# Second dense product cut 384 + 256 columns in place of 512 + 128, with two 256-wide pieces to a PSUM bank

## The chip, the cores and the metric

One core of one Trainium2 chip. The metric is the device time of one execution in microseconds. Engines are written as the profile writes them: PE is the tensor engine, PEld its weight loads, DVE the vector engine, ACT the scalar engine.

## The reference

A gate mixes two branches over 2048 tokens of 640 features: a state-space layer (branch A) and a two-layer perceptron (branch B). Only the last line of branch B is touched here.

```python
g = sigmoid((x * gate_w).sum(-1, keepdims=True))
a = state_space(x, ...)                       # two complex products and a scan over time
h = gelu(x @ w1 + b1)                         # 640 -> 1728: first dense product
b = h @ w2 + b2                               # 1728 -> 640: second dense product
out = g * a + (1 - g) * b                     # bfloat16, 1 x 2048 x 640
```

## The kernel before

The tokens are taken in four chunks of 512, each of four tiles of 128 tokens. PE runs the products of the chunks one after the other in a fixed order; ACT and DVE keep up beside it. In the second dense product the weight tile (the stationary operand) is a 128 x 128 piece of the hidden activations, `gel`, and `w2` streams past it. The matmuls write into banks of PSUM that the program allocates 512 columns wide, and none of them writes more, so the 640 output columns are taken in two pieces. There are 13 full contraction blocks of 128 and a last one of 64 rows, which is done in `half_rows` with two 64-row matmuls side by side.

```python
MAIN, REST = (0, 512), (512, D)               # D = 640

def biased(c, kind, i):                       # ACT writes the bias b2 into a PSUM bank ahead of the product
    p = bank()                                # one of 8 banks, in rotation
    d0, d1 = MAIN if kind == "wide" else REST
    n = 1 if kind == "wide" else H            # H = 2: two REST pieces share a bank
    ...
    nc.scalar.activation(out=v, in_=src, func=ACT.Identity)
    act(0.6 if n == 1 else 0.4)               # the scheduler's own clock; it only decides the order of issue
    opened[c, kind, i] = p

def first_banks(c):                           # called before the product in front ends
    biased(c, "wide", 0)
    biased(c, "wide", 1)

def fin_b(c, at={}):
    def full(p, col, a, d0, d1):
        for kf in range(KF - 1):              # 13 blocks
            nc.tensor.matmul(p[:, col:col + d1 - d0], lhsT=gel[c][:, kf, a * P:(a + 1) * P],
                             rhs=w2_sb[:, kf, d0:d1], start=False, stop=False, skip_group_check=True)
            pe(d1 - d0)
    def out_of(p, col, a, d0, d1):            # eviction by ACT, times (1 - g)
        ...
    def half_rows(): ...                      # the last 64 rows, all four tiles, once per chunk
    biased(c, "rest", 0)
    biased(c, "wide", 2)
    for h in range(2):
        for j in range(H):
            a = h * H + j
            full(opened[c, "wide", a], 0, a, *MAIN)
            if a == 0:
                biased(c, "wide", 3)
                biased(c, "rest", 1)
            if h == 1:
                out_of(opened[c, "wide", a], 0, a, *MAIN)
            ...
        for j in range(H):
            full(opened[c, "rest", h], j * P, h * H + j, *REST)
        if h == 0:
            half_rows()
            ...                               # evictions of the wide pieces
        ...                                   # evictions of the rest pieces
```

`full` is line 598, `half_rows` 614, `biased` 587, `out_of` 606. The changed kernel has one line more, so there they are 599, 615, 588 and 607. Three words: the third product is the last one of a chunk (line 657, the states of the scan times C); a seed is a DVE write of x times D into a bank ahead of it (line 573); a fold is a one-off scaling of C.

## Time and profile before

| | |
|---|---|
| time, median of 3 runs | 215.77 us (215.67 to 216.65) |
| PE / DVE / ACT busy | 98% / 88% / 48% |
| granted PE clock (share of full speed) | 1.0 |
| matmuls at line 598, mean distance of starts | 215.8 to 216.0 ns (512 wide), 55.8 ns (128 wide) |
| the second dense product (lines 598 and 614) | 28% of the chain that ended last |

First the engine line of the page, and the two lines of the chain that ended last: the work followed back from the last instruction, at each step to what released it (shares of the span, by engine and by line).

```profile
PE 210.0 (98%) x1385; PEld 116.4 (54%) x1385; DVE 188.4 (88%) x385; ACT 103.3 (48%) x185; POOL 1.1 (0%) x12
...
PE 96%; DMA 2%; SPq 0%; ACT 0%; DVE 0%; issue 0%
PE bank L598 27%; PE bank L258 26%; PE bank L657 20%; PE bank L540 20%; DMA xn<-in_A_x_dram 2%; PE bank L614 1%; PE bank L284 1%; PE bank L223 0%; SPq L122 0%; ACT xT L232 0%; DVE ot L662 0%; PE bank L361 0%; PE bank L274 0%; PE bank L390 0%
```

A busy PE alone says little, since matmul records overlap. The chain says more: nearly all of the time is PE following itself. The next lines are PE's waits in the trace before (total us, times, longest): 1.5 us in all, every one in the first 8 us.

```profile
PE bank L220 <- PEq L716: 0.8, 1, 0.8
PE bank L361 <- ACT xT L232: 0.3, 1, 0.3
PE bank L223 <- DMA xn<-in_A_x_dram: 0.2, 1, 0.2
PE bank L258 <- DVE xT L230: 0.2, 1, 0.2
```

Now the chain in order of time (start us, length us, what, number of instructions) around the products of the last chunk.

```profile
185.69 7.06 PE bank L598 x52
192.76 0.65 PE bank L614 x8
193.41 7.17 PE bank L598 x52
200.58 10.90 PE bank L657 x90
```

Fifty-two matmuls of the second product (26 of 512 columns, 26 of 128) take 7.06 us, so a pair takes 271.5 ns. Last, the groups by shape: busy us, mean ns of one, then idle time before them.

```profile
L598 PE MATMUL bank<-w_sb,gel 128*128 128x512 bf16 x208 | 46.2, 379 | 0.0
L598 PEld LDWEIGHTS <-gel 128*128 128x128 bf16 x416 | 32.3, 98 | 25.5
L598 PE MATMUL bank<-w_sb,gel 128*128 128x128 bf16 x208 | 12.9, 219 | 0.0
L606 ACT ACTIVATE gb<-bank,gcol 128x512 f32<-128x512 f32 x16 | 10.6, 686 | 30.3 <-PE bank L614 17.3 <-PE bank L598 12.9
L587 ACT ACTIVATE bank<-b2bc 128x512 f32<-128x512 bf16 x16 | 9.1, 599 | 6.1 <-DVE ot L662 6.1
L606 ACT ACTIVATE gb<-bank,gcol 128x128 f32<-128x128 f32 x16 | 5.0, 368 | 3.2 <-PE bank L598 3.2
L587 ACT ACTIVATE bank<-b2bc 128x256 f32<-128x256 bf16 x8 | 3.1, 389 | 1.2 <-DVE ot L662 1.2
```

A weight load shows 98 ns. A 128-wide matmul starts 55.8 ns after the one before it, and each has a load of its own. But 98 ns is how long one load's record is, not how often loads can follow each other: matmuls with a load each did follow each other at 55.8 ns (200 distances, all 55 or 56), with no idle time before them. (The starts are taken from the instruction records of the trace.)

### The profile page before, as it was taken

To read this page: it belongs to the slowest core of one execution; us is meant where nothing else is said; L and a number is where in the kernel's file an instruction comes from. 1 tells how busy PE (TensorE), PEld (TensorE's weight loads), DVE (VectorE), ACT (ScalarE), POOL (GpSimd) and SP (SyncE) were. 2 spreads that over 40 slices of the span, in tenths; PEclk is the share of its full clock that TensorE was granted. 3 is DMA by queue.
4 is the path that set the end of the run, shared out by engine and by line. 5 is a ranking of instruction groups with operands and counts; after the bars stand their busy time and mean duration, and the time that the engine had idled before them with its cause. 6 is when DMAs were issued, how large, how long until landed. Compare 5 with 4: busy or idle time off the path is not lost.

```text
span 214.2 us, 3547 instructions
## 1 busy us (share of the span) xinstructions
PE 210.0 (98%) x1385; PEld 116.4 (54%) x1385; DVE 188.4 (88%) x385; ACT 103.3 (48%) x185; POOL 1.1 (0%) x12
## 2 busy tenths in 40 slices
PE   7999999999999999999999999999999999999994
PEld 3745444454454644775445577444455567664773
DVE  2899999999998999998999999899999999973153
ACT  3599956675867697203573210456682422304200
POOL 1000000000000000000000000000000000000000
PEclk9999999999999999999999999999999999999999
DMA  6899999995000000061000006100000000100011
GB/s 200 238 189 182 187 250 314 257 212 136 3 0 0 3 0 2 12 186 62 0 0 3 0 0 185 63 0 0 2 3 14 0 3 31 61 34 0 0 66 61
DMA packets 31059, 15.84 MB, mean 74 GB/s; under 512 B 22978, under 2 KB 31042, under 8 KB 31042
## 3 DMA queue, kind: packets, MB, share of 16 engines
q1 hardware_dynamic: 30590, 15.18, 29.1%
q10 hardware_dynamic: 452, 0.43, 0.6%
q8 instruction: 11, 0.18, 0.3%
q14 instruction: 6, 0.05, 0.1%
HBM read 7.48 MB, written 2.62 MB: 47 GB/s over the span
## 4 chain that ended last, share of the span: by engine, by line
PE 96%; DMA 2%; SPq 0%; ACT 0%; DVE 0%; issue 0%
PE bank L598 27%; PE bank L258 26%; PE bank L657 20%; PE bank L540 20%; DMA xn<-in_A_x_dram 2%; PE bank L614 1%; PE bank L284 1%; PE bank L223 0%; SPq L122 0%; ACT xT L232 0%; DVE ot L662 0%; PE bank L361 0%; PE bank L274 0%; PE bank L390 0%
## 5 line engine op out<-in xcount | busy, mean ns | idle before, releaser
L598 PE MATMUL bank<-w_sb,gel 128*128 128x512 bf16 (+1 forms) x416 | 57.9, 299 | 0.0
L598 PEld LDWEIGHTS <-gel 128*128 128x128 bf16 x416 | 32.3, 98 | 25.5
L543 ACT ACTIVATE bu<-bank 128x512 bf16<-128x512 f32 x40 | 23.6, 608 | 37.3 <-PE bank L540 36.7
L263 ACT ACTIVATE gel<-bank,colB 128x512 bf16<-128x512 f32 x52 | 33.9, 696 | 11.7 <-PE bank L258 11.4
L657 PEld LDWEIGHTS <-hs 128*128 128x128 bf16 x330 | 31.6, 98 | 11.5
L494 DVE TENSOR_TENSOR_SCAN g<-r_c,carry,v 128x512 bf16<-128x512 f32 x30 | 37.3, 1271 | 0.0
L606 ACT ACTIVATE gb<-bank,gcol 128x512 f32<-128x512 f32 (+1 forms) x32 | 15.1, 527 | 33.5 <-PE bank L614 17.3
L258 PE MATMUL bank<-xT,w1a 128*128 128x512 bf16 (+1 forms) x156 | 27.6, 329 | 0.2 <-DVE xT L230 0.2
L657 PE MATMUL bank<-CT_im,hs 128*128 128x320 bf16 (+2 forms) x165 | 27.1, 295 | 0.0
L657 PE MATMUL bank<-CT_re,hs 128*128 128x320 bf16 (+2 forms) x165 | 27.1, 295 | 0.0
L662 DVE SCALAR_TENSOR_TENSOR ot<-bank,gcol,gb 128x320 bf16<-128x320 f32 (+2 forms) x33 | 17.6, 535 | 10.8 <-PE bank L657 10.0
L540 PE MATMUL bank<-xT,BT_re 128*128 128x512 bf16 x100 | 24.8, 379 | 0.0
L540 PE MATMUL bank<-xT,BT_im 128*128 128x512 bf16 x100 | 24.8, 379 | 0.0
L258 PEld LDWEIGHTS <-w1a 128*128 128x128 bf16 x156 | 13.4, 97 | 13.0 <-issue 0.7
L573 DVE TENSOR_TENSOR bank<-xn,Dbc 128x320 f32<-128x320 bf16 (+2 forms) x33 | 14.6, 483 | 3.9 <-ACT gb L606 3.8
L258 PE MATMUL bank<-xT,w1b 128*128 128x512 bf16 x80 | 17.9, 379 | 0.0
L540 PEld LDWEIGHTS <-BT_im 128*128 128x128 bf16 x100 | 9.8, 98 | 11.8
L475 DVE TENSOR_TENSOR v<-wa,wb 128x512 bf16<-128x512 bf16 x40 | 15.2, 421 | 0.6
L540 PEld LDWEIGHTS <-BT_re 128*128 128x128 bf16 x100 | 9.7, 98 | 11.0
L587 ACT ACTIVATE bank<-b2bc 128x512 f32<-128x512 bf16 (+1 forms) x24 | 11.7, 529 | 7.3 <-DVE ot L662 7.3
L475 DVE TENSOR_TENSOR wa<-TCOS,g 128x1024 bf16<-128x1024 bf16 x20 | 13.7, 686 | 0.1
L258 PE MATMUL bank<-xT,w1c 128*128 128x512 bf16 x60 | 13.7, 379 | 0.0
(101 smaller groups left out, 164.2 us busy)
## 6 DMA issues: line engine op xcount, KB each, us to landing
out_dram<-ot SPq DMA_DIRECT2D x15, 160.0 KB, 1.8
w_sb<-in_B_w_dram SPq DMA_DIRECT2D x1, 2080.0 KB
xn<-in_A_x_dram SPq DMA_DIRECT2D x2, 640.0 KB
xn<-in_A_x_dram SPq DMA_DIRECT2D x4, 160.0 KB, 3.7
w1b<-in_B_w_dram SPq DMA_DIRECT2D x5, 128.0 KB, 3.1
xn<-in_A_x_dram SPq DMA_DIRECT2D x2, 320.0 KB, 3.7
w1a<-in_B_w_dram SPq DMA_DIRECT2D x3, 192.0 KB, 3.0
w1c<-in_B_w_dram SPq DMA_DIRECT2D x5, 112.0 KB, 3.5
```

Of the source, the lines that this page charges most:

```text
L258: nc.tensor.matmul(p[:, t0:t1], lhsT=w, rhs=xT[c][:, kd, t0:t1], start=(kd == 0) if first is None else first, stop=(kd == last), skip_grou ...
L263: nc.scalar.activation(out=gel[c][:, kf, :], in_=p[:, :], func=ACT.Gelu_apprx_tanh, bias=b1_c[:, kf:kf + 1])
L475: nc.vector.tensor_tensor(out=o, in0=a, in1=b, op=op)
L494: nc.vector.tensor_tensor_scan(s["g"][:, ri, :], r_c[:, ks:ks + 1].to_broadcast([P, CH]), s["v"][:, ri, :], init, ALU.mult, ALU.add)
L540: nc.tensor.matmul(p[:], lhsT=BT[ks >= KSA][:, kd, (ks % KSA if ks < KSA else ks - KSA) * P:][:, 0:P], rhs=xT[c][:, kd, :], start=(kd == 0 ...
L543: nc.scalar.activation(out=bu[:, ri, :], in_=p[:], func=ACT.Identity)
L573: dve_now(ck.pe, 0.45, lambda: nc.vector.tensor_tensor(out=p[:, 0:d1 - d0], in0=xn[c][:, a, d0:d1], in1=Dbc[:, d0:d1], op=ALU.mult))
L587: nc.scalar.activation(out=v, in_=src, func=ACT.Identity)
L598: nc.tensor.matmul(p[:, col:col + d1 - d0], lhsT=gel[c][:, kf, a * P:(a + 1) * P], rhs=w2_sb[:, kf, d0:d1], start=False, stop=False, skip_ ...
L606: nc.scalar.activation(out=gbs[ti][:, d0:d1], in_=p[:, col:col + d1 - d0], func=ACT.Identity, scale=gcol[:, 1, ti:ti + 1])
L657: nc.tensor.matmul(p[:, 0:d1 - d0], lhsT=hs[c][:, j, lo:lo + P], rhs=CT[:, j % KS, d0:d1], start=False, stop=(j == 2 * KS - 1), skip_group ...
L662: nc.vector.scalar_tensor_tensor(out=ot[:, d0:d1], in0=p[:, 0:d1 - d0], scalar=gcol[:, 0, ti:ti + 1], in1=gbs[ti][:, d0:d1], op0=ALU.mult, ...
```

## The change

The intent, as far as the edit shows it: replace a wide and a very narrow piece by two of middling width, so that no matmul is so short that its weight load can't hide behind it. 384 + 256 is the most even cut for which two narrow pieces still share one bank of 512 columns, so that the number of open banks stays at six per chunk.

```diff
-    MAIN, REST = (0, 512), (512, D)
+    WIDE = 3 * P
+    MAIN, REST = (0, WIDE), (WIDE, D)
...
-        act(0.6 if n == 1 else 0.4)
+        act(0.5 if n == 1 else 0.6)
...
-            act(0.7 if d1 - d0 > 320 else 0.4)
+            act(0.56 if d1 - d0 > 320 else 0.45)
...
-                        p, col = (opened[c, "wide", h * H + j], 0) if d0 == 0 else (opened[c, "rest", h], j * P)
+                        p, col = (opened[c, "wide", h * H + j], 0) if d0 == 0 else (opened[c, "rest", h], j * (D - WIDE))
...
-                full(opened[c, "rest", h], j * P, h * H + j, *REST)
+                full(opened[c, "rest", h], j * (D - WIDE), h * H + j, *REST)
...                                           (and the same offset in the eviction)
```

More of the change, by code (lines that the diff above doesn't have):

```diff
@@ L639, in fin_b @@
             for j in range(H):
-                out_of(opened[c, "rest", h], j * P, h * H + j, *REST)
+                out_of(opened[c, "rest", h], j * (D - WIDE), h * H + j, *REST)
             let_out(ck.pe)
```

## The prediction

The 5.2 us in the text below is an estimate from the 81 ns of the Trainium skill that it quotes, made only to be set aside: the trace before shows 55.8.

> **What bounds the kernel.** The tensor engine. The page gives PE 98% busy, but matmul records overlap, so I go by the chain of waits and by distances between starts. The chain is 96% PE: from 7.9 to 211.5 us an unbroken row of matmuls. The view of waits lists four PE waits, 1.5 us in all, all before 8 us. The granted clock is 1.0. VectorE is 88% busy, ScalarE 48%.
>
> **What the change does.** In the second dense product (L598, L614) each token tile's 640 columns were cut 512 + 128 and become 384 + 256. The order view shows the same counts: 416 matmuls and 416 weight loads at L598, 32 and 32 at L614, 24 bias writes, 32 evictions. Total columns are unchanged on every engine. Only widths and the moments at which pieces finish move; a few VectorE instructions (folds, seeds) change places.
>
> **PE cost.** The plausible intent is to hide a weight load (98 ns in the groups) behind a wider matmul. The trace says there is nothing to hide. In the matmul records, 128-wide matmuls at L598 start 55.8 ns apart (200 gaps, all 55 or 56), 512-wide ones 215.8 to 216.0. Both lie on one line, 0.417 ns per column plus 2.5 ns, as do the 320-wide (135.8) and 192-wide (82.4) ones at L657. On it 384 costs 162.5 and 256 costs 109.2: 271.7 ns, against 215.8 + 55.8 = 271.6. The chain agrees: 52 matmuls take 7.06 us, 26 x 271.5 ns. The Trainium skill ("TensorE: Matmul & The Clock Gate", Back-to-back issue gap) gives about 81 ns per 128-wide matmul in a stream with weight loads; were that so, the change could save up to 25 x 208 = 5.2 us. This trace shows 55.8, so I expect 0. The switches into and out of the 64-row pieces (gaps of 151 and 148 ns) stay. PE: 0.0 +- 0.1 us.
>
> **ScalarE.** Evictions take 686 ns (512) and 368 (128): 0.828 ns per column. Estimates: 580 (384) and 474 (256), the same sum, 1054. Bias writes of 599 (512, x16) and 389 (256, x8) become 494 (384, x16) and 599 (two pieces, x8): 12.7 us before and after. The last pair of evictions after a product grows from 0.63 to about 0.86 us, the wide ones end 0.7 us earlier: both off the critical path.
>
> **Slack that absorbs the reordering.** The last scan result is written at 190.8 us, read from 200.6. Seeds wait for evicted banks (3.8 us on VectorE, in the last chunk), but its first four are ready 3 us before PE needs them. Hence no new PE wait, and the tail (9.9 us of third product, one vector operation, output DMA) is the same.
>
> **Prediction: 215.8 us, 8 in 10 between 215.1 and 216.7.** Faster by over 2%: 0.01; within 2%: 0.97; slower by over 2%: 0.02.
>
> **What would show it right or wrong.** Chain pieces of L598 again 7.06 and 7.17 us per half chunk; L614 0.65 us; starts 162 to 163 and 109 ns apart; PE busy within 0.5 us; no PE wait after 8 us; evictions near 580 and 474 ns.
>
> **What would make it wrong.** A 256-wide piece at column 256 of a bank that streams slower than the line; a PE wait because a bank is freed later (the rest bank by 0.2 us) or because VectorE stalls on an earlier seed or fold. Run-to-run spread (215.67 to 216.65) is larger than any effect that I can name.

## The result

| | before | after |
|---|---|---|
| median of 6 runs, us | 216.19 | 216.08 |
| lowest to highest, us | 215.67 to 216.81 | 215.75 to 216.33 |
| ratio of fast runs | | 0.9992 (95%: 0.9969 to 1.0015) |
| the same again (experiment 10) | 215.77 | 215.72, ratio 0.9998 (0.9977 to 1.0020) |

A ratio is the mean time of one kernel's fast runs over that of the other's in the same rounds, so it is not quite the ratio of the medians. The times are the same: the narrower interval leaves room for a gain of at most 0.23%. The output passed the comparison with the reference in all twelve experiments, the changed kernel among them (experiment 10). That is weak evidence for this product: experiment 4, which leaves out one block in thirteen, passed as well.

The engine line and the two chain lines of the changed kernel:

```profile
PE 210.0 (98%) x1374; PEld 125.4 (58%) x1385; DVE 187.8 (88%) x385; ACT 103.1 (48%) x185; POOL 1.1 (0%) x12
...
PE 98%; issue 0%; ACT 0%; DVE 0%
PE bank L599 27%; PE bank L258 26%; PE bank L658 20%; PE bank L540 20%; PE bank L220 1%; PE bank L615 1%; PE bank L284 1%; PE bank L223 1%; ACT xT L232 0%; DVE ot L663 0%; PE bank L361 0%; PE bank L274 0%; PE bank L390 0%
```

PE is busy for the same 210.0 us (eleven matmul records are missing from this trace, 1374 in place of 1385; the weight loads are all there). PE's waits, all of them at the start as before:

```profile
PE bank L220 <- PEq L717: 0.8, 1, 0.8
PE bank L361 <- ACT xT L232: 0.3, 1, 0.3
```

The chain around the products of the last chunk:

```profile
185.84 7.06 PE bank L599 x52
192.90 0.65 PE bank L615 x8
193.55 7.17 PE bank L599 x52
200.72 10.91 PE bank L658 x90
```

The lengths are those of before to the last digit, but for 0.01 us in the last line. And the groups by shape:

```profile
L599 PEld LDWEIGHTS <-gel 128*128 128x128 bf16 x416 | 40.2, 98 | 17.1 <-issue 0.8
L599 PE MATMUL bank<-w_sb,gel 128*128 128x384 bf16 x208 | 35.2, 327 | 0.0
L599 PE MATMUL bank<-w_sb,gel 128*128 128x256 bf16 x208 | 24.0, 273 | 0.0
L607 ACT ACTIVATE gb<-bank,gcol 128x384 f32<-128x384 f32 x16 | 8.8, 578 | 27.0 <-PE bank L615 19.1 <-PE bank L599 7.9
L588 ACT ACTIVATE bank<-b2bc 128x384 f32<-128x384 bf16 x16 | 7.4, 493 | 4.1 <-DVE ot L663 4.1
L607 ACT ACTIVATE gb<-bank,gcol 128x256 f32<-128x256 f32 x16 | 6.7, 474 | 9.2 <-PE bank L599 9.2
L588 ACT ACTIVATE bank<-b2bc 128x512 f32<-128x512 bf16 x8 | 4.8, 604 | 1.5 <-DVE ot L663 1.5
```

Starts are 162.7 ns (384) and 109.2 ns (256) apart, 271.9 ns for the pair against 271.8 before (216.0 + 55.8). One number did move: weight loads are busy 40.2 us in place of 32.3, although there are 416 of 98 ns in both. Before, loads 56 ns apart overlapped each other and the overlap counts once; now all but five are 108 ns apart or more and don't overlap. It is bookkeeping, not work.

### The profile page after: what moved, and what is told of

Its sections match the earlier page's. It is cut to its first block, busy times and chain, and to the rows that moved or that the text cites. A ratio compares the mean times of both kernels' runs of the same rounds, so it can differ in the third digit from the quotient of the medians.

```text
span 214.4 us, 3536 instructions
## 1 busy us (share of the span) xinstructions
PE 210.0 (98%) x1374; PEld 125.4 (58%) x1385; DVE 187.8 (88%) x385; ACT 103.1 (48%) x185; POOL 1.1 (0%) x12
## 4 chain that ended last, share of the span: by engine, by line
PE 98%; issue 0%; ACT 0%; DVE 0%
PE bank L599 27%; PE bank L258 26%; PE bank L658 20%; PE bank L540 20%; PE bank L220 1%; PE bank L615 1%; PE bank L284 1%; PE bank L223 1%; ACT xT L232 0%; DVE ot L663 0%; PE bank L361 0%; PE bank L274 0%; PE bank L390 0%
## 5 line engine op out<-in xcount | busy, mean ns | idle before, releaser
L599 PE MATMUL bank<-w_sb,gel 128*128 128x384 bf16 (+1 forms) x416 | 57.9, 300 | 0.0
L599 PEld LDWEIGHTS <-gel 128*128 128x128 bf16 x416 | 40.2, 98 | 17.1 <-issue 0.8
L607 ACT ACTIVATE gb<-bank,gcol 128x384 f32<-128x384 f32 (+1 forms) x32 | 15.1, 526 | 36.3 <-PE bank L615 19.1
L588 ACT ACTIVATE bank<-b2bc 128x384 f32<-128x384 bf16 (+1 forms) x24 | 11.7, 530 | 5.6 <-DVE ot L663 5.6
```

Source lines behind the costliest of these rows:

```text
L607: nc.scalar.activation(out=gbs[ti][:, d0:d1], in_=p[:, col:col + d1 - d0], func=ACT.Identity, scale=gcol[:, 1, ti:ti + 1])
```

## The experiments

My theory, A: the cost of a matmul with its load is 0.417 ns per column plus 2.5 ns down to well below 128 columns, so the same columns in the same number of matmuls cost the same. Rivals: narrow pieces are bound by their loads after all (B: 81 ns for a narrow matmul with its load, C: 98 ns), with the gain lost again; a gain on PE doesn't show because something else sets the time (D); the sharing of a bank costs what the widths bring (E); repeated loads cost something that the sum hides (F); G came up after experiment 9, that alternating widths or banks costs PE time. Unless noted, the edit is to the kernel before. The medians of 1 and 9 count their one slow run too (without it they are 218.12 and 219.15); the ratios are of fast runs alone.

| experiment | median us | before, same rounds | ratio (95% interval) |
|---|---|---|---|
| 1 pieces of 128 | 218.23 | 216.42 | 1.0086 (1.0062 to 1.0111) |
| 11 the same again | 217.58 | 215.77 | 1.0073 (1.0057 to 1.0090) |
| 2 pieces of 64 | 220.47 | 216.42 | 1.0196 (1.0175 to 1.0217) |
| 3 pieces of 32 | 274.15 | 216.42 | 1.2680 (1.2652 to 1.2709) |
| 4 one block left out | 211.80 | 216.42 | 0.9795 (0.9777 to 0.9814) |
| 5 loads twice, before | 216.59 | 216.10 | 1.0019 (1.0004 to 1.0033) |
| 6 loads twice, after | 216.16 | 216.10 | 1.0001 (0.9987 to 1.0015) |
| 7 own banks, opened late | 219.42 | 216.10 | 1.0156 (1.0142 to 1.0170) |
| 8 shared bank, opened late | 219.29 | 216.10 | 1.0160 (1.0137 to 1.0182) |
| 9 pieces in turn | 219.22 | 215.77 | 1.0152 (1.0133 to 1.0172) |
| 12 pieces in turn, opened early | 216.42 | 216.19 | 1.0014 (0.9992 to 1.0036) |
| 10 the changed kernel again | 215.72 | 215.77 | 0.9998 (0.9977 to 1.0020) |

### 1 to 3, and 11: narrower and narrower pieces

```diff
     def full(p, col, a, d0, d1):
+        W = 128                               # 64 and 32 in experiments 2 and 3
         for kf in range(KF - 1):
-            nc.tensor.matmul(p[:, col:col + d1 - d0], lhsT=gel[c][:, kf, ...], rhs=w2_sb[:, kf, d0:d1], ...)
             pe(d1 - d0)                       # the scheduler's clock is kept, so the order of issue stays
+        for e0 in range(d0, d1, W):
+            for kf in range(KF - 1):
+                nc.tensor.matmul(p[:, col + e0 - d0:col + e0 - d0 + W], lhsT=gel[c][:, kf, ...], rhs=w2_sb[:, kf, e0:e0 + W], ...)
```

Pieces of 128 were expected to give the following. The 81 ns of rival B is the figure that the prediction quotes from the Trainium skill, and the +28 us is an estimate from it.

> Before's layout, but the 512-wide piece of the second product is streamed as four 128-wide matmuls: 5 matmuls of 128 per weight tile and token tile in place of 2, every one with its own weight load; 208 x 3 = 624 matmuls more, same columns. Theory A (a weight load is hidden even behind 128 columns, a matmul costs 2.5 ns plus 0.417 ns per column): 624 x 2.5 ns = +1.6 us, ratio about 1.007, starts 55.8 ns apart. Rival B (a narrow matmul with its load costs about 81 ns when the stream is long, and the 55.8 ns of before is an artefact of short rows of 26): 5 x 81 - 271.6 = 133 ns x 208 = +28 us. Rival C (a load occupies the array for its 98 ns): +45 us.

Measured: ratio 1.0086. Its profile fell into a run of 247.8 us at a granted clock of 0.853 and tells nothing of sizes, so the kernel was run again:

> The kernel of e1 again, since its profile fell into a run at a granted clock of 0.85: in a fast profile Theory A wants starts of 55.8 ns in all rows of 128-wide matmuls, also in rows of 65, and a ratio of about 1.007 (e1 measured 1.0086, 1.0062 to 1.0111). If the fast profile shows starts above 56 ns, the small excess over 1.007 is a real cost of loads in long narrow rows.

Measured: ratio 1.0073, 1.8 us between the medians, against 1.6 expected. The chain of that fast profile, for a half chunk:

```profile
57.62 7.26 PE bank L602 x130
64.87 0.65 PE bank L617 x8
65.52 7.36 PE bank L602 x130
```

A hundred and thirty matmuls in 7.26 us are 55.8 ns each, in rows of 130 as in rows of 26 (the 65 of the expectation is the count of one token tile). So 55.8 ns is a sustained rate, and B and C, which need 81 or 98 ns, are out.

Pieces of 64:

> Same with pieces of 64 columns: 10 matmuls and 10 loads per weight tile and token tile. Theory A: 10 x 29.2 - 271.6 = 20 ns x 208 = +4.2 us, starts 29 ns apart (the 65-wide matmuls elsewhere in the kernel before average 30.5). Rival C: 10 x 98 - 272, +147 us. A load that needs between 30 and 98 ns would show as a floor under the distance of starts, and the time grows by 208 x (10 x floor - 272) ns.

Measured: ratio 1.0196, that is 4.1 us between the medians against 4.2 expected; starts 29.2 ns apart. Half of the narrow piece's width is still on the line, with five times as many loads as before.

Pieces of 32 (the +47 us of the expectation is an estimate from the floor of the Trainium skill, which is cited with its page below):

> Same with pieces of 32 columns: 20 matmuls and 20 loads per weight tile and token tile. The line alone gives 15.8 ns per matmul and +9.3 us. I expect that here the load, or another fixed cost per pair, is at last the limit: the Trainium skill names a floor of about 25 ns for starts, which would be 20 x 25 - 272 = 228 ns x 208 = +47 us. Whatever floor shows is what a weight load with its matmul costs at least, and tells how far the 128 columns of before were from being load-bound.

Measured: ratio 1.268, 57.7 us between the medians. Here is the floor at last: of 4152 distances at this line, 4111 are 25 ns, where the line alone would give 15.8. The Trainium skill ("TensorE: Matmul & The Clock Gate", Wait — 56ns, not 53.3ns?) states such a floor of about 25 ns for starts of small matmuls, and this trace agrees. The one 15-wide matmul of the kernel before (line 361) was followed after 25 ns too. The floor accounts for 20 x 25 - 272 = 228 ns x 208 = 47 us. The remaining 10 us come from something that I had not expected: once 200 to 400 of these matmuls of a chunk have run, PE pauses at multiples of 128 matmuls with their 128 loads (what the distances have above 25 ns sums to 9.9 us). The chain of this kernel, in the first chunk:

```profile
75.85 3.35 PE bank L602 x128
79.20 0.65 issue
79.85 3.35 PE bank L602 x128
83.20 0.10 issue
83.30 3.35 PE bank L602 x128
86.65 0.38 issue
```

"issue" is time in which the engine waited for nothing that the profile shows. The regular count of 128 pairs suggests the supply of instructions, and the page of this run agrees so far: its instruction queue q8 moved 40 packets, 11 in the kernel before, so 29 more for 7488 more instructions, one per 258 or about 128 pairs. But experiment 2 needed 24 such packets and has no pause, and no view names what PE waited for, so the cause stays open. What matters is the floor: a matmul with its own load took at least 25 ns here, and the narrow piece of before gave it 55.8.

### 4: would a gain on PE show at all?

```diff
-            for kf in range(KF - 1):
+            for kf in range(KF - 2):          # in full(): 12 blocks of 13, result wrong on purpose
```

> Control, result wrong on purpose: before's kernel with 12 of the 13 full contraction blocks in the second product. Theory A (the second product lies on the critical path matmul by matmul): 16 token tiles x 271.6 ns = 4.35 us less, ratio about 0.980. Rival D (the time is set by VectorE or another wait, so that a real gain on the tensor engine would not have shown either): same within 0.3%.

Measured: ratio 0.9795, 4.6 us between the medians (the ratio times 216.4 gives 4.4), against 4.35 expected. The time taken off this product came off the total, within the interval (0.9777 to 0.9814 is 4.0 to 4.8 us). Rival D is out: had the new widths saved PE time, the total would have shown it.

### 5 and 6: every load twice

```diff
+                nc.tensor.ldweights(gel[c][:, kf, a * P:(a + 1) * P])    # in full(), before each matmul
                 nc.tensor.matmul(...)
```

On the kernel before:

> Before's kernel with every weight load of the second product's 416 full matmuls issued twice (same data, so the result stays right). Theory A with a load that needs no more than about 28 ns of the array's load path: two loads still fit behind 128 columns, time within 0.3%. If a load needs about 56 ns or a second load can't be taken up before its matmul starts, the 208 narrow matmuls pay: one extra 30 to 100 ns each, +6 to +21 us, and the wide ones nothing or the same.

On the changed kernel:

> The changed kernel with the same doubling. If loads were close to limiting at 128 columns, this one has more room (109 ns behind 256 columns, 163 behind 384) and grows less than e5 does: this is the case in which the change's intent would pay. Theory A says both grow alike, by 0 if two loads fit everywhere, or by the same fixed cost per extra load if it can't overlap at all.

Measured: ratio 1.0019 and 1.0001. Doubling 416 loads costs the kernel before 0.4 us, and the changed one nothing that the interval can tell from zero. The distances say where: the 128-wide matmuls of experiment 5 start 57.7 ns apart in place of 55.8, and 208 x 1.9 ns = 0.4 us; the 512-wide ones keep 216 ns (five distances of 431 or 432 among 192 are missing records), and in experiment 6 the 384- and 256-wide ones keep 162.8 and 109.2. Both kernels also leave the 64-row matmuls 40 ns later (189 ns in place of 148 in experiment 5, 241 in place of 201 in experiment 6), 0.16 us over four chunks, too little to show in the ratios. The loads themselves start 15 and then about 42 ns apart in the narrow rows of experiment 5, though each record is 95 to 98 ns long. My expectation that both grow alike was wrong by this 0.4 us: two loads and a 128-wide matmul need 57.7 ns, just over what 128 columns offer. So the changed widths do have more room for loads, exactly as intended; but with one load per matmul nothing needs the room.

### 7 and 8: the shared bank

Experiment 7 gives each 256-wide piece of the changed kernel a bank of its own. That makes eight open banks per chunk, so the first two can't be opened ahead of time any more. Experiment 8 opens them as late but keeps the sharing.

```diff
 # both
-    ssm(1, {KS - 1: lambda: first_banks(0)})
+    ssm(1)
     gates(1)
+    first_banks(0)                            # likewise for chunks 1 and 2
 # experiment 7 also
-        n = 1 if kind == "wide" else H
+        n = 1
-                full(opened[c, "rest", h], j * (D - WIDE), h * H + j, *REST)
+                full(opened[c, "rest", h * H + j], 0, h * H + j, *REST)      # likewise in half_rows and eviction
```

> The changed widths with one PSUM bank for each 256-wide piece (8 banks open per chunk in place of 6, hence the first two can only be opened after the product before has let its own go). Theory: sharing costs nothing by itself (matmuls 109 ns apart in either case), but without it the early opening is lost and PE waits for ScalarE at the start of chunks 0 to 2, about 1.3 to 2 us each: +3 to +5 us against before. Rival E (two 256-wide pieces in one bank slow the matmuls or delay something, and that hid a gain of the widths): faster than the changed kernel and than before.

> The changed kernel (shared bank) with the first two banks opened as late as in e7, so that the two differ in the sharing alone. Theory: the same time as e7 within 0.3%, i.e. +3 to +5 us against before, all of it PE waiting on ScalarE's bias writes. Rival E: slower than e7.

Measured: ratio 1.0156 and 1.0160, the same within their intervals. PE's new wait is the same line in both profiles; this is experiment 7's:

```profile
PE bank L599 <- ACT bank L588: 3.1, 3, 1.1
```

and the chain at the start of its first product shows what PE waits for, the bias written by ACT:

```profile
46.58 10.75 PE bank L540 x49
57.33 0.02 issue
57.35 0.02 ACT bu L543
57.38 0.47 issue
57.85 0.50 ACT bank L588
58.34 0.04 issue
58.39 7.22 PE bank L599 x52
```

Three waits of 3.1 us in all explain most of the 3.2 to 3.3 us between the medians. The 256-wide matmuls start 109.2 ns apart with and without sharing. Rival E is out: sharing costs nothing by itself, and what it buys is the early opening. This is why the rest piece could not be wider than 256: two would not fit one bank.

### 9 and 12: both pieces of a tile in turn

The changed kernel, but for each weight tile the 384-wide and then the 256-wide matmul, so that two matmuls in a row need the same weights.

```diff
-                full(opened[c, "wide", a], 0, a, *MAIN)
+                for kf in range(KF - 1):
+                    for p, col, d0, d1 in ((opened[c, "wide", a], 0, *MAIN), (opened[c, "rest", h], j * (D - WIDE), *REST)):
+                        nc.tensor.matmul(p[:, col:col + d1 - d0], lhsT=gel[c][:, kf, ...], rhs=w2_sb[:, kf, d0:d1], ...)
...
-                full(opened[c, "rest", h], j * (D - WIDE), h * H + j, *REST)
```

> The changed kernel with the two pieces of a token tile taken in turn: for each weight tile the 384-wide and then the 256-wide matmul, so that two matmuls in a row use the same weight tile. Same matmuls, same columns. Theory A: the order of the pieces and the repeated weights mean nothing, time within 0.3% of the changed kernel, starts 162.5 and 109.2 ns apart; if the compiler or the chip leaves out the repeated load, half the loads are gone and the time still stays. Rival F (loads cost something that the sum hides): up to 1% faster when loads are left out or repeat.

Measured: ratio 1.0152, a clear miss. The profile was of no use: it fell into a run of 1264 us in which PE's 320-wide matmuls stood 843 ns apart in place of 136. Experiments 7 and 8 offered a reason, and the last kernel tested it:

```diff
 def first_banks(c):
     biased(c, "wide", 0)
-    biased(c, "wide", 1)
+    biased(c, "rest", 0)                      # and the other way round at the start of fin_b
```

> e9 came out 3.3 us slower than before against my expectation of no change, and its profile fell into a run of 1264 us and can't be used for sizes. My reading: taking the pieces in turn needs the shared bank of 256-wide pieces from the first pair on, and e9 opened it only at the start of the product, so that PE waited for ScalarE in chunks 0 to 2 as in e7 and e8 (3 x 1.1 us). Here that bank is opened early in place of the second wide bank, nothing else differs from e9. If the reading is right: ratio 1.000 within 0.003, starts 162.5 and 109.2 ns apart, no PE wait in the product. Rival G (alternating banks or widths costs PE about 16 ns per pair, 208 x 16 ns = 3.3 us): again 1.015, with starts whose sum per pair is about 287 ns.

Measured: ratio 1.0014 (0.9992 to 1.0036); starts 162.7 and 109.2 ns apart, a pair at 271.9 ns; PE's waits are only the two of the start, and the chain has its usual lengths:

```profile
186.09 7.06 PE bank L627 x52
193.15 0.65 PE bank L615 x8
193.80 7.17 PE bank L627 x52
```

So the 3.4 us of experiment 9 were, but for a small rest, the bank that was opened late, and rival G is out. All 416 loads are still in the trace (none was left out), so a version with half the loads was not had, and rival F is only answered for repeated loads. The small rest, 0.2 us between the medians, is within the interval; the trace has one distance of 373 ns in place of 136 between two matmuls of the third product, which the chain leads back to DVE, and that alone would be 0.24 us.

### 10: the changed kernel again

> The changed kernel unchanged, once more with more rounds and on another chip perhaps, because the first interval (0.9969 to 1.0015) would still allow a gain of 0.3%. Theory A: ratio 1.000 within 0.002. Any rival that sees a gain of the wider pieces: below 0.998.

Measured: 0.9998 (0.9977 to 1.0020), with the chain at 7.06, 0.65 and 7.17 us in all four chunks. No experiment pointed to a version that beats both kernels.

## Why the prediction was right

- **Bound by PE.** Right, and shown by experiment 4: 4.35 us of matmuls taken away took about that much off the total.
- **A narrow matmul is not bound by its load.** Right. The prediction read it from 55.8 ns at 128 columns and from the common line through 512, 320, 192 and 128 columns; experiments 2, 3 and 11 carry the line on to 64 columns and find the floor of 25 ns below it.
- **Widths.** Predicted 162.5 and 109.2 ns, measured 162.7 and 109.2; the chain's 7.06, 7.17 and 0.65 us came back unchanged.
- **ACT.** Predicted evictions of 580 and 474 ns, measured 578 and 474; bias writes 494 and 599 ns, measured 493 and 604. The last pair of evictions was expected at about 0.86 us, and the timeline of the changed kernel has it at 0.84. The last two wide evictions end 0.66 and 1.35 us earlier (196.39 for 197.05, 198.50 for 199.85), where the prediction has 0.7 for both. None of it mattered, since PE never waited for it.
- **Slack.** Right. DVE's wait for banks before its seeds grew from 3.8 to 4.9 us, and no PE wait came of it. The 9.9 us that the prediction gives for the third product in the tail is a slip: the chain has 10.90 before and 10.91 after, and nothing rests on it. Experiments 7 and 8 show what it looks like when the slack is used up: PE waits 3.1 us for ACT, and the time grows by 3.2 to 3.3 us.
- **Time.** Predicted 215.8 (215.1 to 216.7), measured 216.08. The 0.3 us between them is in the kernel before as well: 215.77 over the three runs that the prediction knew, 216.19 over six.

The claim about the intent, that it was to hide the loads, remains a reading of the edit. Experiment 5 shows how near the case is to one where it would pay: with two loads per matmul the narrow piece loses 1.9 ns each, and the new widths lose nothing.

## What to carry to other kernels

The length of an instruction's record is not the interval at which such instructions can follow each other: before reshaping matmuls to hide weight loads, measure the distance of their starts at several widths and see whether they lie on one line. If a product streams on that line, as here, only fewer columns or fewer matmuls shorten it. And in a kernel where PE never waits, a change of tiling is judged by what it does to the moment at which banks can be opened, not by the busy time of the other engines.

## What the Trainium skill lacked or had wrong

- "TensorE: Matmul & The Clock Gate", Back-to-back issue gap, gives about 81 ns per matmul at N=128 and 131 ns at N=512 for a stream of loads and matmuls, and calls N/2.4 + 2.5 ns the isolated gap. Here the stream with a load for each matmul ran at 55.8 ns (128) and 215.8 ns (512): the formula holds in the stream, and down to 64 columns (29.2 ns).
- The same page, LDWEIGHTS, gives the time of a load as columns / 1.2, 107 ns for 128; its table in Weight-path perf modes gives 32 cycles in theory, for fp8, and about twice the plain speed as measured. The record here shows 98 ns, yet loads with their matmuls followed each other 25 ns apart in experiment 3, and two loads with a 128-wide matmul took 57.7 ns in experiment 5. The page does not tell the length of the record from the interval.
- "Perfetto Trace Analysis", Identifying the Most-Contended Engine, names the sum of the weight loads' slices over the window, beside the share of peak arithmetic, as a measure of how close PE is to its roofline. By that sum both kernels stand at 63 to 64% (135.7 of 214.2 us, 136.3 of 214.4), and experiment 3, which is 27% slower, at 181% (493.3 of 271.9 us), because load records overlap. The page doesn't say that the sum can pass 100%. The busy share printed in the profile counts an overlap once, and so it rose from 54% to 58% with the same 1385 loads and the same time.
- "TensorEngine Tiling (Array Packing)", Key Properties, says that a change of tiling mode drains PE, without a cost. Here entering the 64-row mode took 151 ns after a 128-wide matmul in place of 55.8, and 204.5 after a 256-wide one in place of 109.2: about 95 ns.
- The 1264 us run of experiment 9 (320-wide starts 843 ns apart in place of 136) was recorded with a granted clock of 1.0. "TensorE: Matmul & The Clock Gate", Seeing it yourself, warns that the trace's clock events can be unreliable and tells of a clock stuck at a quarter for over 50 us; the distances here are 6.2 times as long (843 over 136), and the cause is open.
- No page that I read has the pauses of 0.1 to 0.65 us at multiples of 128 load and matmul pairs of experiment 3. "Runtime: NRT & Kernel Launch", Instruction fetch mechanics, has the block size that would fit, 256 instructions, and says that crossing a block is mostly hidden; here the pauses come to about 10 us, if that is their cause, which is not shown.
